# Value products over 128 rows for the last eight heads of a fused attention and feed-forward kernel

## The chip, the cores and the metric

The kernel runs on one core of a Trainium2 chip. The metric is the device time of one execution in microseconds (us), as a median of several runs. A core has a matrix engine (PE, with its weight loads shown as PEld), a vector engine (DVE), a scalar engine (ACT), a general engine (POOL) and an engine that mostly issues transfers (SP). Each works through its own queue in order; semaphores tie them together. Products are written to PSUM, eight banks of 512 f32 columns by 128 partitions; all else lies in SBUF.

## What is computed

The input x has 2048 rows of 512 columns. Part A is attention with 32 heads of 16 columns, in which a query sees itself and the 255 keys before it. Part B picks the 8 rows with the largest x @ w_r and adds a gated feed-forward result to them. The output mixes both by a gate for each row.

```python
qkv = x @ wqkv                              # 32 heads of 16
scores = einsum(q, k) * 16 ** -0.5          # mask: 0 <= i - j < 256
o = softmax(scores) @ v
a = o @ wo
r = x @ w_r;  idx = argsort(-r)[:8]
y = (silu(x[idx] @ w_gate) * (x[idx] @ w_up)) @ w_down
b = x;  b[idx] += y * sigmoid(r[idx])
out = g * a + (1 - g) * b                   # g = sigmoid(sum(x * gate_w))
```

## The kernel before

**Work and stages.** The 32 heads are four quarters c = 0 to 3 of eight heads, the 2048 rows are 16 row blocks j of 128 and 64 key blocks kb of 32. The scores are computed transposed: a product with the block-diagonal keys `Kbd` as weights and the queries `QT` as moving operand gives, for the 32 keys of one block, four heads on 128 partitions (head by key) and up to 256 query columns. The eight heads of a quarter are two sets s = 0, 1 of four heads; the products of set 0 use rows 0 to 63 of the PE array, those of set 1 rows 64 to 127 (`tile_position=(64 * s, 0)`), so that the two run side by side. One such group of score products is a *unit* (`unit`, L640 to L680): products at L658 into one of two pairs of banks of `psS`, an exponential on ACT at L669 that writes the weights `PT`, and a mask of the triangle at L680 on DVE or POOL. "M" units hold two key blocks, "T" units the last 32 query columns of eight. Quarters 0 and 1 go one after the other, 2 and 3 are interleaved by row block.

**Value products** (`pv`, L687). For each row block, key block and set s, `PT` (128 partitions of head and key, 128 queries) is the weight operand, and the values `Vbd` move. The 128 partitions are cut into halves r of two heads, one half a product of 64 rows and 34 columns (two heads of 16 values and a column of ones, which yields the softmax denominator), into bank r of `psO` (L699). `Vbd` has two buffers, one for c % 2 = 0 and one for 1. A value tile is made from a projection in `psG` (`v_tail`, L600): a transpose on DVE to the single buffer `VT` (L603) and two multiplications with a 0/1 column (L607, DVE or POOL) that put each head's values in its rows.

**Normalisation** (`norm`, L717). Of each batch of row blocks DVE takes the reciprocal of the denominators (L726), multiplies it with the gate (L738), and scales `psO` into `On` (L742). A DMA transposes `On` into `OT` (L772); for row blocks 14 and 15 of quarters 2 and 3 PE transposes it into a bank of `psG` (L759), and DVE (L767) or ACT (L764) copies it to `OT`. `outp` (L777) multiplies with `wo` (L793; L790 for blocks 14 and 15, over 128 rows), combines with (1 - g) * b on DVE (L798; block 15 adds it by a product, L785, and ACT copies, L796), and stores.

**Other work on PE.** Projections of q, k, v (L621, L628) into two banks of `psG`; gate and up products of the feed-forward part (L873, 112 products of 8 columns with weights in `big`), down products (L915, 14 products of 512 columns); a few filler products (L541, L545), which write nothing that is used.

**The end.** Every reciprocal is checked against limits, in two pieces of 480 and 32 columns (L1041 to L1043); two small products (L1048) sum the result, DVE writes `flag` (L1051), and all engines read it (L1182) and branch past a general version of the kernel (L1184).

**Order.** The order of every engine's queue is a table of numbers (`ORDER`, L1105; `BANK` and `FILL` beside it), one number for each operation in the order in which the program makes them. `Sched.schedule` puts the queues together by it and adds the waits. An operation that stands ahead in a queue and waits holds up all behind it.

## Time and profile before

| what | value |
|---|---|
| time before, median of 3 runs | 173.4 us (173.19 to 173.93) |
| the profiled execution | 172.88 us |
| its span, first to last instruction | 171.3 us |
| PE busy (modelled) | 157.3 us, 92%, 4575 products |
| DVE busy | 119.7 us, 70% |
| ACT busy | 138.3 us, 81% |
| POOL busy | 67.3 us, 39% |

In the groups of the profile each row has line, engine, operation, output and inputs, shapes and count; then busy us and mean ns of one; then the engine's idle time before these instructions, and what ended it. "64*128 64x34" is a product with a weight operand of 64 rows by 128 columns and 34 moving columns. In the timeline a row has start, length and count of like instructions that stand together. Products overlap in PE's pipeline: one lasts some 170 ns, but the next starts long before its end.

### The profile page before, as it was taken

How to read it: one execution, taken by the hardware profiler on the slowest of the kernel's cores; microseconds unless marked ns; L12 is line 12 of the kernel's file. 1: busy time of each engine (PE TensorE's matmuls, PEld its weight loads, DVE VectorE, ACT ScalarE, POOL GpSimd, SP SyncE). 2: the span in 40 equal slices, each digit the busy share in tenths (PEclk: the TensorE clock that was granted, in tenths of full speed). 3: DMA queues.
4: the chain of work that ended last, by engine and by line, in shares of the span. 5: the costliest groups of instructions: out<-in, count | busy, mean ns of one | idle time of the engine just before them, and what ended most of it. 6: DMA issues, size and time to landing. Idle time of an engine off the chain costs nothing. (4 is left out here: it accounts for less than half of the span.)

```text
span 171.3 us, 10022 instructions
## 1 busy us (share of the span) xinstructions
PE 157.3 (92%) x4575; PEld 108.2 (63%) x4575; DVE 119.7 (70%) x328; ACT 138.3 (81%) x171; POOL 67.3 (39%) x130
## 2 busy tenths in 40 slices
PE   4989999999999999999997999999999999689960
PEld 1447767766474776778783567576777587476520
DVE  7694899997684418687885756888974657568750
ACT  2277889999999879898999669999999989847120
POOL 2100364750793894202518143524353244246000
PEclk9999999999999957999999999999999999999997
DMA  6994194644677442440328532028110434424621
GB/s 131 216 229 104 18 247 84 154 108 110 154 188 125 125 84 65 139 136 13 96 72 151 188 64 67 4 67 159 32 65 4 103 90 127 122 88 109 188 86 53
DMA packets 35745, 18.68 MB, mean 109 GB/s; under 512 B 27616, under 2 KB 35568, under 8 KB 35568
## 3 DMA queue, kind: packets, MB, share of 16 engines
q1 hardware_dynamic: 34560, 17.71, 42.7%
q8 instruction: 36, 0.59, 1.5%
q10 hardware_dynamic: 1072, 0.26, 0.7%
q0 software_dynamic: 64, 0.02, 0.3%
q14 instruction: 13, 0.11, 0.2%
HBM read 11.81 MB, written 4.20 MB: 93 GB/s over the span
## 5 line engine op out<-in xcount | busy, mean ns | idle before, releaser
L669 ACT ACTIVATE f_PT<-f_psS 128x1024 bf16<-128x1024 f32 (+3 forms) x156 | 132.3, 918 | 16.2 <-PE f_psS L658 14.2
L680 POOL TENSOR_TENSOR f_PT<-f_PT,f_MK 128x128 bf16<-128x128 bf16 (+1 forms) x83 | 41.5, 513 | 83.7 <-ACT f_PT L669 79.8
L658 PE MATMUL f_psS<-f_QT,f_Kbd 64*128 64x256 bf16 (+3 forms) x960 | 65.4, 225 | 1.2 <-ACT f_PT L669 0.7
L628 PE MATMUL f_psG<-f_XT,f_W 64*128 64x512 bf16 x360 | 65.8, 379 | 0.3
L699 PEld LDWEIGHTS f_psO<-f_Vbd,f_PT 64*128 64x128 bf16 x2880 | 54.3, 93 | 10.3 <-DVE f_On L742 3.5
L699 PE MATMUL f_psO<-f_Vbd,f_PT 64*128 64x34 bf16 x2880 | 58.4, 174 | 2.2 <-DVE f_On L742 1.2
L658 PEld LDWEIGHTS f_psS<-f_QT,f_Kbd 64*128 64x128 bf16 x960 | 32.1, 94 | 19.1 <-ACT f_PT L669 10.6
L628 PEld LDWEIGHTS f_psG<-f_XT,f_W 64*128 64x128 bf16 x360 | 20.7, 93 | 9.9 <-PE f_psG L628 0.9
L793 PE MATMUL f_psG<-f_wo,f_OT 64*128 64x512 bf16 x112 | 22.9, 376 | 1.2 <-DVE f_outt L798 1.2
L680 DVE TENSOR_TENSOR f_PT<-f_PT,f_MK 128x128 bf16<-128x128 bf16 (+1 forms) x73 | 19.5, 285 | 4.7 <-ACT f_PT L669 4.5
L587 DVE TENSOR_SCALAR f_Kbd<-f_Kr,f_hm 128x512 bf16<-128x512 bf16 (+2 forms) x62 | 20.9, 374 | 1.9 <-ACT f_Kr L575 1.6
L798 DVE SCALAR_TENSOR_TENSOR f_outt<-f_xr,f_omg_f,f_psG 128x512 bf16<-128x512 bf16 x15 | 11.2, 744 | 8.6 <-PE f_psG L793 3.0
L575 DVE CAST f_QT<-f_psG 128x512 bf16<-128x512 f32 (+1 forms) x15 | 10.0, 664 | 6.9 <-PE f_psG L628 6.1
L603 DVE STREAM_TRANSPOSE f_VT<-f_psG 128x512 f32<-128x512 f32 x16 | 11.4, 712 | 3.3 <-PE f_psG L628 2.7
L607 POOL TENSOR_SCALAR f_Vbd<-f_VT,f_pb 128x512 bf16<-128x512 f32 x16 | 11.6, 729 | 2.5 <-DVE f_VT L603 2.3
L742 DVE TENSOR_TENSOR f_On<-f_psO,f_RG 128x512 bf16<-128x512 f32 (+1 forms) x17 | 11.2, 657 | 1.6 <-DMA f_OT<-f_On 1.1
L726 DVE RECIPROCAL f_RC<-f_psO 128x32 f32<-128x32 f32 (+1 forms) x17 | 5.8, 343 | 8.2 <-PE f_psO L699 8.1
L575 DVE CAST f_Kr<-f_psG 128x512 bf16<-128x512 f32 x12 | 8.2, 686 | 3.4 <-PE f_psG L628 3.2
L587 POOL TENSOR_SCALAR f_Kbd<-f_Kr,f_hm 128x512 bf16<-128x512 bf16 (+1 forms) x6 | 8.5, 1420 | 5.1 <-ACT f_Kr L575 5.1
L793 PEld LDWEIGHTS f_psG<-f_wo,f_OT 64*128 64x128 bf16 x112 | 7.6, 93 | 4.2 <-DVE f_outt L798 1.9
L607 DVE TENSOR_SCALAR f_Vbd<-f_VT,f_pb 128x512 bf16<-128x512 f32 x16 | 8.6, 549 | 0.1
L534 PE MATMUL f_psS<-f_RC 128*128 128x512 bf16 x10 | 3.9, 544 | 2.4 <-DVE f_pb L472 2.4
(106 smaller groups left out, 70.0 us busy)
## 6 DMA issues: line engine op xcount, KB each, us to landing
f_xc<-in_A_x_dram SPq DMA_DIRECT2D x8, 256.0 KB, 3.4
f_xr<-f_xc SPq DMA_DIRECT2D x16, 128.0 KB, 2.6
out_dram<-f_outt SPq DMA_DIRECT2D x16, 128.0 KB, 2.2
f_big<-in_B_w_gate_dram SPq DMA_DIRECT2D x8, 224.0 KB, 3.0
f_big<-in_B_w_up_dram SPq DMA_DIRECT2D x8, 224.0 KB, 3.6
f_OT<-in_B_w_down_dram SPq DMA_DIRECT2D x4, 256.0 KB, 3.8
f_W<-in_A_wqkv_dram SPq DMA_DIRECT2D x2, 384.0 KB, 3.9
f_xr<-in_B_w_down_dram SPq DMA_DIRECT2D x2, 256.0 KB, 4.1
```

The lines of the kernel that those rows point to most:

```text
L575: return e.copy(out=o, in_=i) if e is nc.scalar else e.tensor_copy(out=o, in_=i)
L587: add("dve", lambda e, h=h: e.tensor_scalar(out=Kbd[:, sl, a // 32:(a + n) // 32, h, :], in0=Kr[:, kr, a:a + n].rearrange("p (a k) -> p a ...
L603: add("dve", lambda e: e.transpose(out=VT[:], in_=psG[:, it.r, :]), item=it, w=[("VT", vb)], occ=630, due=due, cls="ev")
L607: add(VENG, lambda e, o=o, i=i, b=b: e.tensor_scalar(out=o, in0=i, scalar1=pb_[:, b:b + 1], scalar2=1.0, op0=ALU.mult, op1=ALU.mult), r=[( ...
L628: return e.matmul(psG[:, it.r, 0:n], W[P, kc, which, 128 * c:128 * c + 128], XT[P, kc, 512 * tc + a:512 * tc + a + n], start=(k8 == 0), st ...
L658: ins[s] = e.matmul(psS[:, sb2 + s, n * k:n * k + n], Kbd[P, kslot[(c, kb // 16)][0], kb % 16].rearrange("p h k -> p (h k)"), QT[P, c % 2, ...
L669: add("act", lambda e: e.activation(out=oa, in_=ia, func=ACT.Exp, scale=0.25), r=[("S", i % 2)], w=pk_ + [("ex", i)], occ=2 * nk * n * 0.8 ...
L680: add(eng, lambda e: e.tensor_tensor(out=v, in0=v, in1=m, op=ALU.mult), r=MKR + pk_, w=pk_, occ=cost[eng], due=at(i + 1), cls="mk", alt=(o ...
L699: ins[r] = e.matmul(psO[:, r, 68 * ji + 34 * s:68 * ji + 34 * s + 34], PT[P, s, o0:o0 + 128], Vbd[P, c % 2, s, kb, :], start=(kb == kbs[0] ...
L742: add("dve", lambda e: e.tensor_tensor(out=o, in0=i0_, in1=i1_, op=ALU.mult), r=["O", "RG"], w=[("On", ob, 0), ("On", ob, 1)], occ=60 + 12 ...
L793: return e.matmul(psG[:, it.r, :], OTrun(c, a, 1)[P], wo[P, c, :], start=(k8 == 0), stop=(k8 == 7), tile_position=(64 * x, 0), skip_group_ ...
L798: add("dve", lambda e: e.scalar_tensor_tensor(out=outt[:, xs, :], in0=xr[:, xs, :], scalar=omg_f[:, a:a + 1], in1=psG[:, it.r, :], op0=ALU ...
```

## The change

For quarter 3 alone (`FC = (3,)`) the value products use all 128 rows: `PT` of a set s, whole, is the weight operand, and 68 columns move (four heads of 16 values and a one), into bank s of `psO`. So one product takes the place of two. The value tiles are block-diagonal over four heads, and lie in `big`, where the gate and up weights lay, so they may be written once the gate and up products are done; a tile takes eight multiplications of half the size, four heads times two sets. The ones are written by two fills. The rows of `OT` for quarter 3 then have another order of heads, and the rows of `wo` are loaded accordingly, in two transfers for each of the four.

```diff
+        VF = [[...], [AP(big, 4352 * k, [[14336, 128], [68, 64], [1, 68]]) for k in (1, 2)]]
...
+            if c in FC:
+                for b in range(4):
+                    for s2 in range(2):
+                        add(VENG, lambda e, b=b, s2=s2: e.tensor_scalar(out=VF[c - 2][s2][:, 16 * tc:16 * tc + 16, 17 * b:17 * b + 16],
+                                                                        in0=VT[:].rearrange("p (k f) -> p k f", f=32)[:, :, 16 * s2:16 * s2 + 16],
+                                                                        scalar1=pf_[:, b:b + 1], scalar2=1.0, op0=ALU.mult, op1=ALU.mult),
+                            r=[("VT", vb), ("pf", b), ("Vfone", c, s2)], w=[("Vf", c, tc, b, s2)], occ=420, due=due + 2, cls="vb", alt=("dve", 290))
+                return
...
+        def pvf(c, j, ji, due, kbs):
+            for g in range(0, len(kbs), PVF):
+                part = kbs[g:g + PVF]
+                for s in range(2):
+                    def fn(e, s=s, part=part):
+                        ins = None
+                        for kb in part:
+                            o0 = poff(c, kb) + 128 * j - 32 * kb
+                            ins = e.matmul(psO[:, s, 68 * ji:68 * ji + 68], PT[:, s, o0:o0 + 128], VF[c - 2][s][:, kb], start=(kb == kbs[0]), stop=(kb == kbs[-1]), skip_group_check=True)
+                        return ins
...
+            if c in FC:
+                pvf(c, j, ji, due, kbs)
+                return
...
+PVF = 6
+FC = (3,)
```

The transposes of the last two row blocks go to the score banks (`psS`), block 14 to the first pair and block 15 to the second, no longer to `psG`. They are made at the end of the program, and each output product of these blocks now depends on its own quarter's part of `OT` alone.

```diff
-                it = S.item(None, True)
-
-                def fn(e):
-                    ins = None
-                    for ji in range(n):
-                        ins = e.matmul(psG[:, it.r, 128 * ji:128 * ji + 128], On[:, ob, ji, :], ident[:], start=True, stop=True)
-                    return ins
...
+                def late():
+                    k = j0 % 2
+
+                    def fn(e):
+                        ins = None
+                        for ji in range(n):
+                            ins = e.matmul(psS[:, 2 * k + (ji if k else 0), 128 * ji:128 * ji + 128], On[:, ob, ji, :], ident[:], start=True, stop=True, skip_group_check=True)
+                        return ins
...
+                    if k == 0:
+                        add("dve", lambda e: e.tensor_copy(out=OTrun(2, 14, 2), in_=psS[:, 0, 0:256]), r=[("S", 0)] + ow, w=[("OT", 2, 14), ("OT", 3, 14)], occ=70 + 266, due=due + 100, cls="nm")
+                    else:
+                        add("act", lambda e: e.copy(out=OTrun(2, 15, 1), in_=psS[:, 2, 0:128]), r=[("S", 1)] + ow, w=[("OT", 2, 15)], occ=55 + 107, lat=175 + 107, due=due + 100, cls="nm")
+                        add("dve", lambda e: e.tensor_copy(out=OTrun(3, 15, 1), in_=psS[:, 3, 128:256]), r=[("S", 1)] + ow, w=[("OT", 3, 15)], occ=70 + 133, due=due + 100, cls="nm")
...
-                add("pe", fn, r=[("OT", c, a) for c in ((k8 % 4,) if last else range(4))] + WO, item=it, occ=215, lat=380, due=due, half="f" if tail else 0, cls="op", cw=512 if tail else 256)
+                add("pe", fn, r=[("OT", c, a) for c in ((k8 % 4,) if tail else range(4))] + WO, item=it, occ=215, lat=380, due=due, half="f" if tail else 0, cls="op", cw=512 if tail else 256)
...
-FILL = {13: 33, 15: 3, 18: 1, 37: 33, 39: 1, 53: 17, 61: 1}
+FILL = {4: 1, 18: 1, 54: 33, 79: 1, 107: 1}
```

`ORDER`, `BANK` and `FILL` are new from the first row on, so the order differs in the whole kernel. Three places show it. First PE, in the dense stretch of quarters 2 and 3, before: L658 are scores, L699 value products, L793 output products with `wo`, of four score units in a row.

```order
L658 MATMUL f_psS<-f_QT,f_Kbd 128x256 x4
L793 MATMUL f_psG<-f_wo,f_OT 128x512
L699 MATMUL f_psO<-f_Vbd,f_PT 128x34 x32
L658 MATMUL f_psS<-f_QT,f_Kbd 128x256 x4
L793 MATMUL f_psG<-f_wo,f_OT 128x512 x8
L658 MATMUL f_psS<-f_QT,f_Kbd 128x32 x16
L699 MATMUL f_psO<-f_Vbd,f_PT 128x34 x32
L658 MATMUL f_psS<-f_QT,f_Kbd 128x256 x4
```

The same four units after the change: L679 are scores, L835 output products, L716 full-height value products.

```order
L679 MATMUL f_psS<-f_QT,f_Kbd 128x256 x4
L716 MATMUL f_psO<-f_big,f_PT 128x68 x24
L679 MATMUL f_psS<-f_QT,f_Kbd 128x256 x4
L835 MATMUL f_psG<-f_wo,f_OT 128x512 x8
L716 MATMUL f_psO<-f_big,f_PT 128x68 x24
L679 MATMUL f_psS<-f_QT,f_Kbd 128x32 x16
L835 MATMUL f_psG<-f_wo,f_OT 128x512
L679 MATMUL f_psS<-f_QT,f_Kbd 128x256 x4
```

The full-height products stand in blocks of 24 between lines that use half the rows: there are 16 such blocks, of 6 to 48 products. Second, PE at the down products (L915), before:

```order
L658 MATMUL f_psS<-f_QT,f_Kbd 128x32 x16
L699 MATMUL f_psO<-f_Vbd,f_PT 128x34 x56
L658 MATMUL f_psS<-f_QT,f_Kbd 128x256 x8
L915 MATMUL f_psG<-f_OT,f_HT 8x512 x8
L915 MATMUL f_psG<-f_xr,f_HT 8x512 x4
L915 MATMUL f_psG<-f_scr,f_HT 8x512 x2
L658 MATMUL f_psS<-f_QT,f_Kbd 128x256 x4
```

And after, where L957 are the down products and L739 the half-height value products:

```order
L679 MATMUL f_psS<-f_QT,f_Kbd 128x32 x16
L957 MATMUL f_psG<-f_OT,f_HT 8x512 x4
L679 MATMUL f_psS<-f_QT,f_Kbd 128x256 x8
L739 MATMUL f_psO<-f_Vbd,f_PT 128x34 x8
L957 MATMUL f_psG<-f_OT,f_HT 8x512 x2
L716 MATMUL f_psO<-f_big,f_PT 128x68 x4
L957 MATMUL f_psG<-f_OT,f_HT 8x512 x2
L716 MATMUL f_psO<-f_big,f_PT 128x68 x20
L679 MATMUL f_psS<-f_QT,f_Kbd 128x32 x16
L679 MATMUL f_psS<-f_QT,f_Kbd 128x256 x4
L957 MATMUL f_psG<-f_xr,f_HT 8x512 x4
L957 MATMUL f_psG<-f_scr,f_HT 8x512 x2
```

The 14 products stood in one piece, and now stand in four, with score units between. Third, the end of DVE's queue, before; `f_outt` are the output combinations, `f_scr` and `f_okc` the check of the denominators.

```order
L738 TENSOR_TENSOR f_RG<-f_RC,f_g_f 128x16
L1041 TENSOR_SCALAR f_scr<-f_RC 128x32
L742 TENSOR_TENSOR f_On<-f_psO,f_RG 128x2x2x64
L798 SCALAR_TENSOR_TENSOR f_outt<-f_xr,f_omg_f,f_psG 128x512
L767 CAST f_OT<-f_psG 128x256
L1042 SCALAR_TENSOR_TENSOR f_scr<-f_RC,f_scr 128x32
L798 SCALAR_TENSOR_TENSOR f_outt<-f_xr,f_omg_f,f_psG 128x512
L1043 TENSOR_REDUCE f_okc<-f_scr 128x1
L1051 TENSOR_SCALAR flag<-f_psO 1x1
```

After (L840 are the combinations, L1096 to L1098 the check, L1106 the flag):

```order
L1097 SCALAR_TENSOR_TENSOR f_scr<-f_RC,f_scr 128x32
L782 TENSOR_TENSOR f_On<-f_psO,f_RG 128x2x2x64
L840 SCALAR_TENSOR_TENSOR f_outt<-f_xr,f_omg_f,f_psG 128x512
L807 CAST f_OT<-f_psS 128x128
L840 SCALAR_TENSOR_TENSOR f_outt<-f_xr,f_omg_f,f_psG 128x512
L1098 TENSOR_REDUCE f_okc<-f_scr 128x1
L1096 TENSOR_SCALAR f_scr<-f_RC 128x480
L1097 SCALAR_TENSOR_TENSOR f_scr<-f_RC,f_scr 128x480
L1098 TENSOR_REDUCE f_okc<-f_scr 128x1
L1106 TENSOR_SCALAR flag<-f_psO 1x1
```

The three operations on 480 columns, which stood among earlier work, are now the last ahead of the flag.

78 lines of the change are left out of this document (52 added, 26 removed), and 132 rows, old and new, of the table ORDER.

## The prediction, on record before the changed kernel ran

> **What bounds the kernel now.** I read the page first, for the shares of the span.
>
> ```profile
> span 171.3 us, 10022 instructions
> PE 157.3 (92%) x4575; PEld 108.2 (63%) x4575; DVE 119.7 (70%) x328; ACT 138.3 (81%) x171; POOL 67.3 (39%) x130
> ```
>
> The profiled execution took 172.88 us, so 1.6 us lie around its span; it lies 0.5 us under the median of the runs, 173.4. PE's 92% is modelled time of pipelined products and says little, so I took the busy time by stretches (columns: PE, PEld, DVE, ACT, POOL), and in the dense stretch 100 to 140 us PE's and ACT's groups by form.
>
> ```profile
> 100.00:140.00 40.00, 39.61 (x1292) 27.86 (x1286) 28.57 (x69) 39.42 (x46) 15.43 (x30) 1.00 0.28 67
> 140.00:160.00 20.00, 17.68 (x595) 12.99 (x593) 13.72 (x33) 14.58 (x20) 8.93 (x17) 1.00 0.42 117
> ```
> ```profile
> L628 PE MATMUL f_psG<-f_XT,f_W 64*128 64x512 bf16 x102 | 19.4, 376 | 0.0
> L699 PE MATMUL f_psO<-f_Vbd,f_PT 64*128 64x34 bf16 x856 | 17.2, 174 | 0.2 <-DVE f_On L742 0.2
> L658 PE MATMUL f_psS<-f_QT,f_Kbd 64*128 64x256 bf16 x144 | 15.9, 270 | 0.1
> L793 PE MATMUL f_psG<-f_wo,f_OT 64*128 64x512 bf16 x46 | 11.2, 376 | 0.0
> L658 PE MATMUL f_psS<-f_QT,f_Kbd 64*128 64x32 bf16 x144 | 3.7, 174 | 0.0
> ```
>
> ACT (the exponentials, L669) is busy 39.4 of these 40 us. For PE's real load I need what one product costs in a run, from the first to the last start. The timeline of PE has runs of each kind (start, length, instructions):
>
> ```profile
> 57.72 1.34 PE L873 MATMUL f_psG<-f_xselT,f_big 128*128 128x8 bf16 x48 [0.35 <-issue]
> 58.99 0.39 PE L658 MATMUL f_psS<-f_QT,f_Kbd 64*128 64x256 bf16 x4
> ...
> 96.30 1.89 PE L915 MATMUL f_psG<-f_OT,f_HT 128*8 128x512 bf16 x8
> ...
> 99.84 0.75 PE L699 MATMUL f_psO<-f_Vbd,f_PT 64*128 64x34 bf16 x48
> 100.45 0.59 PE L628 MATMUL f_psG<-f_XT,f_W 64*128 64x512 bf16 x4
> ```
>
> ```profile
> L873 PE MATMUL f_psG<-f_xselT,f_big 128*128 128x8 bf16 x112 | 3.3, 167 | 0.3 <-issue 0.3
> ```
>
> A run of n takes one duration and n-1 steps. L915 (512 columns, 376 ns each as L628's) gives (1.89-0.376)/7 = 0.216 us for 512 columns, 0.42 ns a column. L699 gives (0.75-0.174)/47 = 12.3 ns, so the pair of 64-row products for one key block takes 24.6 ns. A 64-row product shares the array with the other half, so 512 columns cost 0.108 us and 256 cost 0.054. The stretch then holds 148 x 0.108 + 144 x 0.054 + 1000 x 0.0123 = 36.1 us of PE work in 40: ACT sets the pace, and PE has about 3.9 us left, some 10%. From 140 to 160 neither engine is full (17.7 and 14.6 of 20): there the waits of the closing blocks decide.
>
> **The end.** The chain of waits on the page is short, so I read the last instructions in the timeline and the line of the final branch (q marks a sequencer; min/median/max in ns).
>
> ```profile
> 162.39 0.42 DVE L742 TENSOR_TENSOR f_On<-f_psO,f_RG 128x256 bf16<-128x256 f32 x1
> 162.76 0.75 DVE L798 SCALAR_TENSOR_TENSOR f_outt<-f_xr,f_omg_f,f_psG 128x512 bf16<-128x512 bf16 x1
> 163.43 0.42 DVE L767 CAST f_OT<-f_psG 128x256 bf16<-128x256 f32 x1
> ...
> 165.03 0.75 DVE L798 SCALAR_TENSOR_TENSOR f_outt<-f_xr,f_omg_f,f_psG 128x512 bf16<-128x512 bf16 x1 [1.09 <-issue]
> 165.70 0.18 DVE L1043 TENSOR_REDUCE f_okc<-f_scr 128x1 f32<-128x32 f32 x1
> 166.23 0.15 DVE L1051 TENSOR_SCALAR flag<-f_psO 1x1 int32<-1x1 f32 x1 [0.35 <-PE f_psO L1048]
> ```
> ```profile
> 163.57 0.29 PE L759 MATMUL f_psG<-f_ident,f_On 128*128 128x128 bf16 x2 [0.68 <-DVE f_outt L798]
> 163.90 1.04 PE L790 MATMUL f_psG<-f_wo,f_OT 128*128 128x512 bf16 x4
> ...
> 164.99 1.03 PE L790 MATMUL f_psG<-f_wo,f_OT 128*128 128x512 bf16 x4
> 165.95 0.24 PE L1048 MATMUL f_psO<-f_ones_f,f_okc 128*1 128x1 f32 x4
> ```
> ```profile
> L1184 PEldq COMPARE_BRANCH  x1: 4133/4133/4133, 167.1 to 167.1; - x1
> ```
>
> The flag (L1051) is ready at 166.38, PE reads it and branches at 167.1, and that branch lasts 4.13 us, to 171.26: it is the span's last event. The last output's copy and store have ended before. So the end hangs on the flag, and the flag on DVE's check of the denominators.
>
> **The change part by part.** *Value products.* 720 half-height products of 34 columns, 720 x 12.3 ns = 8.9 us of PE, become 360 full-height ones of 68 columns. The trace has none of that shape. By L915's 0.42 ns a column one takes 28.7 ns; a little issue time on top makes 29 to 31, together 10.4 to 11.2 us. I take 10.9: +2.0 us of PE work, not a saving. The Trainium skill, page "TensorE: Matmul & The Clock Gate", Part 1, states that starts of successive products never come closer than about 25 ns, however few the columns; by that the old pair would take 50 ns and the edit would save 360 x 19 ns = 6.8 us. The row of 48 in 0.75 us shows 12.3 ns for products that alternate between the halves, so the trace disagrees and I go by the row.
>
> *Switches between 64 and 128 rows.* The first score product after the 48 L873 starts at 58.99, when the last of them, begun at 57.72+1.34-0.167 = 58.89, is only 0.07 us from its end: a step of 0.10 us. Between two half-height lines, L699 to L628 at 100.45, the last start was 100.42: 0.03 us. A switch lets the array run empty, for some 0.07 to 0.10 us. In PE's order, counted from the end of the gate and up products on, 3 switches become 37, around 16 blocks of full-height value products and the pieces of the down products: 34 x 0.09 = 3.1 us. With the products the second half gets +5.1 us of PE work (4.0 to 5.7). Its cover is PE's idle time under ACT, 3.9 us in 100 to 140, where by time some 3.3 of the 5.1 fall, and the idle time after 140. PE would then be at 39.4 of 40: as full as ACT, which waits for scores in the same queue. So not all of it can hide; but not all shows either. I take a quarter, **+1.3 us**, ends 0 and +5.1.
>
> *The first half* loses work: up to the end of the gate and up products 19 switches become 13, and 4 of 9 filler pieces of 240 columns (0.1 us each) go, some 0.9 us of PE in all. But ACT gets four evacuations of 512 Q columns for one and two of K for three, +2 x 0.586 us by
>
> ```profile
> L575 ACT CAST f_QT<-f_psG 128x512 bf16<-128x512 f32 x1 | 0.6, 586 | 0.2 <-PE f_psG L628 0.2
> ```
>
> These cancel as far as I can tell: **0**, ends -1.0 and +1.0.
>
> *The down products* stand in one piece before, 96.30 to 99.47, and ACT waits behind them:
>
> ```profile
> 99.87 1.51 ACT L669 ACTIVATE f_PT<-f_psS 128x1024 bf16<-128x1024 f32 x2 [1.57 <-PE f_psS L658]
> ```
>
> They are now in four pieces with scores between. PE's work is the same, so half of that wait may go: **-0.7**, ends 0 and -1.6.
>
> *Value tiles.* Eight multiplications a tile instead of two, at half the size: 8 before at 549 ns (DVE) or 729 (POOL), 32 after at no less than half of that.
>
> ```profile
> L607 POOL TENSOR_SCALAR f_Vbd<-f_VT,f_pb 128x512 bf16<-128x512 f32 x16 | 11.6, 729 | 2.5 <-DVE f_VT L603 2.3
> ...
> L607 DVE TENSOR_SCALAR f_Vbd<-f_VT,f_pb 128x512 bf16<-128x512 f32 x16 | 8.6, 549 | 0.1
> ```
>
> That is 17 x 0.3 + 15 x 0.4 = 11 us for 5, but over two engines at 28.6 and 15.4 of 40. Masks of 8 blocks move to POOL in exchange (DVE 20 to 14), so DVE keeps its load. What waits behind a tile is the next value transpose, which needs the single f_VT: nothing, ends 0 and +0.8. The two fills of ones on POOL and four more stores of f_wo on SP lie beside idle time: nothing.
>
> *The end.* The transposes of row block 15 no longer wait for a bank of f_psG (0.68 us), and two of block 14's products run ahead of them: after f_On (162.81) the transposes end near 163.2, two products of block 14 near 163.7, and the last L798 near 164.5 instead of 165.78, 1.3 us earlier. That f_On comes later by about 0.5: a second 32-column check stands ahead of it on DVE (0.18), the full-height block takes 0.15 longer than 48 pairs' worth, the transposes of block 14 stand in front (0.15). Against this, the three checks of 480 columns move from among the earlier work to the very end of DVE, behind the last L798:
>
> ```profile
> L1042 DVE SCALAR_TENSOR_TENSOR f_scr<-f_RC,f_scr 128x480 f32<-128x480 f32 x1 | 0.8, 762 | 0.0
> ...
> L1043 DVE TENSOR_REDUCE f_okc<-f_scr 128x1 f32<-128x480 f32 x1 | 0.6, 593 | 0.0
> ...
> L1041 DVE TENSOR_SCALAR f_scr<-f_RC 128x480 f32<-128x480 f32 x1 | 0.4, 403 | 0.0
> ```
>
> 1.76 us more ahead of the flag, of which 0.15 lay under PE's last products before: +1.6. Queued behind the flag is PE's long branch. Sum: +1.6 - 1.3 + 0.5 = **+0.8**, ends -0.8 (the branch is not the end after all, and the earlier store counts) and +1.3.
>
> **Sum.** 1.3 + 0 - 0.7 + 0 + 0.8 = +1.4 us: 174.3 against 172.88 of the profiled execution, **174.8** against the median.
>
> **The rivals.** *The new order recovers idle time (faster).* Before, ACT waits 14.2 us for scores in all,
>
> ```profile
> ACT f_PT L669 <- PE f_psS L658: 14.2, 21, 1.6
> ```
>
> and 4.8 of these lie after 140 us. If the other order closes 3 us of them and the extra PE work stays under ACT, the sum is -3 + 0.8 = -2.2: 171.2; with two of them 172.2. I give 0.32. Against it: at 98% real load in the dense stretch PE has little room to make up for anything. *Everything cancels* (0.26): PE's additional work stays hidden but for 0.5, the down products give 0.7, the end costs 0.5: 173.7. *Weights not hidden (much slower).* If each full-height weight load waits for the product in flight, 360 x 0.025 (L873's whole step of (1.34-0.167)/47 = 25.0 ns, load included) adds up to 9 us; with a third of that, +3, the total is 177.8. The Trainium skill, the same page, Part 3 (The mechanism), has such a rule: loads overlap products in flight only when the row groups differ. L873 loads 128 x 128 weights for every product in the same rows and still steps in 25 ns, so I give 0.05. *The quarter is too small (slower):* the score products come late in each block, and half of the 5.1 us shows, 1.3 more: 176.1; this is in the forecast's upper range.
>
> **How the numbers follow.** My forecast, slower by some 1.4 us, has 0.37, its own range 174.3 to 177.0. With the rival of weights slower has 0.42, no change 0.26, faster 0.32, taking 0.5% (0.87 us) as what a measurement of this kernel can tell. The range 171.2 to 177.2 leaves out the best part of the first rival and the worst of the third.
>
> **What would show it.** In the profile after: the full-height value products in steps of 29 to 31 ns; steps of 0.1 us at each switch; ACT's waits for scores longer between 100 and 140 us, and none of 1.5 us at the down products; the flag later after the last combination by about 1.7 us, and the branch of 4.1 us still last. Wrong it would be if ACT's waits shrink, if the products step in 25 ns or in over 40, or if the branch ends elsewhere.

## The result: slower by 3%, and the profile after

The changed kernel takes 178.76 us (median of 4 runs, 177.79 to 179.52) against 173.34 us (4 runs, 173.19 to 173.93) beside it: ratio 1.0303, 95% interval 1.0247 to 1.0359. On another chip it was 178.45 against 173.46 us, ratio 1.0270 (1.0227 to 1.0313). The profiled execution took 178.69 us with a span of 177.1, where the kernel before had 171.3: 5.86 us to explain, of which 1.4 were foretold. On most of the chips used below the runs of one kernel spread over several us, and the kernel before, loaded a second time, came out at 1.0113 of itself (1.0049 to 1.0178); so differences under about 1% are read from stages of the profiled executions, which mostly repeat between the 61st and the 141st exponential: the one from the 93rd to the 117th took 22.43 or 22.44 us in ten profiles with full-height products. From the 141st to the end of the last exponential they don't repeat: 16.87 and 18.06 us in the two profiles of the changed kernel.

The page after: the head of it, the costliest line of ACT, and the two lines of the full-height value products.

```profile
span 177.1 us, 9324 instructions
...
PE 160.7 (91%) x4208; PEld 108.3 (61%) x4209; DVE 124.8 (70%) x343; ACT 138.8 (78%) x173; POOL 77.1 (44%) x145
...
L690 ACT ACTIVATE f_PT<-f_psS 128x1024 bf16<-128x1024 f32 (+3 forms) x156 | 132.3, 919 | 19.4 <-PE f_psS L679 17.8
```
```profile
L716 PE MATMUL f_psO<-f_big,f_PT 128*128 128x68 bf16 x360 | 14.4, 194 | 0.0
L716 PEld LDWEIGHTS f_psO<-f_big,f_PT 128*128 128x128 bf16 x360 | 12.3, 97 | 4.4 <-issue 4.0 <-DVE f_Kbd L600 0.4
```

ACT does the same 132.3 us of exponentials and waits 19.4 us between them (16.2 before). Where it waits is seen in the table by stage, cut at the starts of the 1st, 53rd, 77th, 93rd, 117th, 121st and 141st exponential, the last one's end and the span's end. Each row: the stretch, its length, the time that exponentials took in it (those cut by a bound are counted in both), the TensorE clock granted, DMA. Before:

```profile
8.61:59.45 50.84, 44.92 (x52) 1.00 0.61 137
59.45:83.70 24.25, 20.45 (x25) 0.86 0.32 85
83.70:100.79 17.09, 13.74 (x16) 1.00 0.49 119
100.79:121.49 20.70, 20.50 (x25) 1.00 0.37 81
121.49:124.94 3.45, 3.35 (x5) 1.00 0.00 0
124.94:142.86 17.92, 17.25 (x21) 1.00 0.28 76
142.86:159.59 16.73, 12.11 (x17) 1.00 0.40 113
159.59:171.26 11.67, 0.00 (x0) 0.91 0.31 101
```

And after:

```profile
8.77:58.08 49.31, 44.43 (x53) 1.00 0.58 134
58.08:85.92 27.84, 20.91 (x25) 0.88 0.25 72
85.92:101.18 15.26, 13.14 (x17) 1.00 0.65 166
101.18:123.61 22.43, 20.95 (x26) 1.00 0.22 56
123.61:128.11 4.50, 3.37 (x6) 1.00 0.01 4
128.11:146.77 18.66, 17.26 (x21) 1.00 0.36 77
146.77:163.64 16.87, 12.21 (x17) 1.00 0.43 124
163.64:177.12 13.48, 0.00 (x0) 0.84 0.27 84
```

The differences of the lengths: -1.53, +3.59, -1.83, +1.73, +1.05, +0.74, +0.14 and +1.81 us; with the first exponential 0.16 later they make the 5.86. The stretch with the down products (77th to 93rd) became shorter, and the next one, in which 96 of the 360 full-height products stand, longer by about as much. The other large losses are the stretch around the gate and up products (53rd to 77th), four exponentials at 124 to 128 us, and the tail behind the last exponential.

### The profile page after: what moved, and what is told of

It is laid out like the page before. It is cut to its first block, busy times and chain, and to the rows that moved or that the text cites. A ratio compares the mean times of both kernels' runs of the same rounds, so it can differ in the third digit from the quotient of the medians.

```text
span 177.1 us, 9324 instructions
## 1 busy us (share of the span) xinstructions
PE 160.7 (91%) x4208; PEld 108.3 (61%) x4209; DVE 124.8 (70%) x343; ACT 138.8 (78%) x173; POOL 77.1 (44%) x145
## 4 chain that ended last, share of the span: by engine, by line
PE 64%; ACT 9%; DVE 9%; issue 7%; POOL 5%; DMA 2%; SPq 1%; POOLq 0%; DVEq 0%
PE f_psG L649 18%; PE f_psS L679 17%; PE f_psO L739 12%; ACT f_PT L690 8%; PE f_psO L716 6%; PE f_psG L835 6%; POOL f_PT L701 3%; DMA f_OT<-f_On 2%; PE f_psG L957 2%; PE f_psG L915 2%; DVE f_PT L530 1%; POOL f_big L1048 1%; DVE f_On L782 1%; DVE f_RG L778 1%; PE f_psG L861 1%
## 5 line engine op out<-in xcount | busy, mean ns | idle before, releaser
L690 ACT ACTIVATE f_PT<-f_psS 128x1024 bf16<-128x1024 f32 (+3 forms) x156 | 132.3, 919 | 19.4 <-PE f_psS L679 17.8
L701 POOL TENSOR_TENSOR f_PT<-f_PT,f_MK 128x128 bf16<-128x128 bf16 (+1 forms) x85 | 45.7, 553 | 69.8 <-ACT f_PT L690 69.6
L679 PE MATMUL f_psS<-f_QT,f_Kbd 64*128 64x256 bf16 (+2 forms) x960 | 65.4, 226 | 1.9 <-ACT f_PT L690 0.9
L649 PE MATMUL f_psG<-f_XT,f_W 64*128 64x512 bf16 x360 | 63.1, 378 | 0.1
L739 PE MATMUL f_psO<-f_Vbd,f_PT 64*128 64x34 bf16 x2160 | 45.7, 174 | 2.8 <-POOL f_PT L701 0.8
L739 PEld LDWEIGHTS f_psO<-f_Vbd,f_PT 64*128 64x128 bf16 x2160 | 41.9, 93 | 9.5 <-DVE f_On L782 2.6
L679 PEld LDWEIGHTS f_psS<-f_QT,f_Kbd 64*128 64x128 bf16 x960 | 31.4, 94 | 21.7 <-ACT f_PT L690 8.1
L701 DVE TENSOR_TENSOR f_PT<-f_PT,f_MK 128x128 bf16<-128x128 bf16 (+1 forms) x71 | 20.6, 305 | 11.1 <-ACT f_PT L690 10.9
L600 DVE TENSOR_SCALAR f_Kbd<-f_Kr,f_hm 128x512 bf16<-128x512 bf16 (+2 forms) x63 | 21.6, 381 | 1.8 <-ACT f_Kr L588 1.2
L835 PE MATMUL f_psG<-f_wo,f_OT 64*128 64x512 bf16 x112 | 21.1, 376 | 1.5 <-issue 0.9
L840 DVE SCALAR_TENSOR_TENSOR f_outt<-f_xr,f_omg_f,f_psG 128x512 bf16<-128x512 bf16 x15 | 11.2, 746 | 7.5 <-PE f_psG L835 3.8
L616 DVE STREAM_TRANSPOSE f_VT<-f_psG 128x512 f32<-128x512 f32 x16 | 11.4, 712 | 5.5 <-PE f_psG L649 5.3
L716 PEld LDWEIGHTS f_psO<-f_big,f_PT 128*128 128x128 bf16 x360 | 12.3, 97 | 4.4 <-issue 4.0
L716 PE MATMUL f_psO<-f_big,f_PT 128*128 128x68 bf16 x360 | 14.4, 194 | 0.0
L588 DVE CAST f_QT<-f_psG 128x512 bf16<-128x512 f32 (+1 forms) x12 | 7.8, 653 | 6.5 <-PE f_psG L649 6.4
L835 PEld LDWEIGHTS f_psG<-f_wo,f_OT 64*128 64x128 bf16 x112 | 7.0, 93 | 5.2 <-issue 1.2
L620 POOL TENSOR_SCALAR f_big<-f_VT,f_pf 128x256 bf16<-128x256 f32 x15 | 7.9, 541 | 1.6 <-DVE f_VT L616 1.5
```

The costliest lines, as they stand in the source:

```text
L588: return e.copy(out=o, in_=i) if e is nc.scalar else e.tensor_copy(out=o, in_=i)
L600: add("dve", lambda e, h=h: e.tensor_scalar(out=Kbd[:, sl, a // 32:(a + n) // 32, h, :], in0=Kr[:, kr, a:a + n].rearrange("p (a k) -> p a ...
L616: add("dve", lambda e: e.transpose(out=VT[:], in_=psG[:, it.r, :]), item=it, w=[("VT", vb)], occ=630, due=due, cls="ev")
L649: return e.matmul(psG[:, it.r, 0:n], W[P, kc, which, 128 * c:128 * c + 128], XT[P, kc, 512 * tc + a:512 * tc + a + n], start=(k8 == 0), st ...
L679: ins[s] = e.matmul(psS[:, sb2 + s, n * k:n * k + n], Kbd[P, kslot[(c, kb // 16)][0], kb % 16].rearrange("p h k -> p (h k)"), QT[P, c % 2, ...
L690: add("act", lambda e: e.activation(out=oa, in_=ia, func=ACT.Exp, scale=0.25), r=[("S", i % 2)], w=pk_ + [("ex", i)], occ=2 * nk * n * 0.8 ...
```

## The experiments

**The end: is it the checks?** *Checks early.* On DVE the three 480-column checks go from behind the last combination to between earlier ones:

```diff
- recip(15), check32, On(15), combine, combine, reduce32, check480 x3, flag
+ mask, check480, combine, check480, combine, check480, recip(14), ... combine, reduce32, flag
```

> The changed kernel with the three 480-column checks moved on VectorE from behind the last combination to the places between the combinations some 10 us earlier, where VectorE waits anyway. Theory (the checks hold the flag, and the branch behind the flag is the last event): the 1.7 us that the three take (0.40, 0.66 and 0.65 us) go from the end, 177.0 us, within 176.7 to 177.4. Rival (something else ends as late as the flag: the last store or TensorE's own queue): 178.4 to 178.8.

Measured: profiled run 176.90 us, span 175.2; ratio 1.0165 (1.0084 to 1.0246). The tail of DVE after, and then that of this run:

```profile
169.35 0.75 DVE L840 SCALAR_TENSOR_TENSOR f_outt<-f_xr,f_omg_f,f_psG 128x512 bf16<-128x512 bf16 x1 [0.45 <-DMA f_xr<-f_xc]
...
170.11 0.40 DVE L1096 TENSOR_SCALAR f_scr<-f_RC 128x480 f32<-128x480 f32 x1
...
170.55 0.66 DVE L1097 SCALAR_TENSOR_TENSOR f_scr<-f_RC,f_scr 128x480 f32<-128x480 f32 x1
171.24 0.65 DVE L1098 TENSOR_REDUCE f_okc<-f_scr 128x1 f32<-128x480 f32 x1
...
172.22 0.15 DVE L1106 TENSOR_SCALAR flag<-f_psO 1x1 int32<-1x1 f32 x1 [0.33 <-PE f_psO L1103]
```
```profile
168.90 0.75 DVE L840 SCALAR_TENSOR_TENSOR f_outt<-f_xr,f_omg_f,f_psG 128x512 bf16<-128x512 bf16 x1
...
170.25 0.15 DVE L1106 TENSOR_SCALAR flag<-f_psO 1x1 int32<-1x1 f32 x1 [0.52 <-PE f_psO L1103]
```

From the last combination's end to the flag's it is 2.27 us after and 0.75 here; from the last exponential's end to the span's end 13.48 and 11.59, about as in the kernel before (11.67). The branch on PE stays the last event.

*The kernel before with the checks late*, the one edit the other way round:

> The kernel before with one thing of the change: the three 480-column checks stand on VectorE behind the last combination and ahead of the flag. Theory (the flag and the branch behind it are the end): from the last exponential's end to the span's end 11.7 us become 13.3 to 13.5, the time 174.9 to 175.2 us against 173.3. Rival (the 1.7 us are hidden in the kernel before): 173.2 to 173.6 us.

Measured: ratio 1.0045 (0.9932 to 1.0157), which tells nothing; TensorE fell to half clock in the tail of the profiled execution (14.27 us of tail). The step itself can be read, since it is DVE's: from the combination's end to the flag's end 168.22 to 170.49, 2.27 us, where the kernel before has 0.59 (165.78 to 166.37).

```profile
167.47 0.75 DVE L798 SCALAR_TENSOR_TENSOR f_outt<-f_xr,f_omg_f,f_psG 128x512 bf16<-128x512 bf16 x1 [1.80 <-issue]
...
170.34 0.15 DVE L1051 TENSOR_SCALAR flag<-f_psO 1x1 int32<-1x1 f32 x1 [0.33 <-PE f_psO L1048]
```

So the checks cost 1.5 us in the changed kernel (2.27 less 0.75) and 1.7 us in the kernel before.

**58 to 86 us: the fills of ones.** GpSimd after, in the timeline: a fill (L1048) stands ahead of masks (L701); the second fill, at 70.54 us, does too.

```profile
66.61 1.28 POOL L1048 CAST f_big<-f_pf 128x256 bf16<-128x256 f32 x1
...
67.95 2.64 POOL L701 TENSOR_TENSOR f_PT<-f_PT,f_MK 128x128 bf16<-128x128 bf16 x3
```

And PE's waits from 58 to 86 us, after:

```profile
PE f_psO L739 <- POOL f_PT L701: 0.8, 2, 0.6
PE f_psO L739 <- DVE f_PT L701: 0.7, 1, 0.7
```

All three, 1.5 us, are waits for masks. Two are for masks of GpSimd, behind the fills in its queue. The third is for a mask of DVE, which no fill holds:

```profile
75.17 1.28 DVE L701 TENSOR_TENSOR f_PT<-f_PT,f_MK 128x128 bf16<-128x128 bf16 x1
```

It lies beside a GpSimd mask of 1.14 us (75.23 to 76.37), one of those that came later because of the fills, and ends 0.08 us behind it. In the run with fills and tile moved the same DVE mask took 0.29 us. So a fill here also did harm by what it pushed beside DVE's work. Three places were tried for the fills:

```diff
  POOL: ... mask | fill | copy, masks | fill | copy, masks, tiles, masks (76.4) | idle 2.6 | tile, mask (80.4) | 68-column tile
- fills at both first bars
+ fills_later: at "idle 2.6";  fills_80: ahead of the 68-column tile
+ fills_and_tile: as fills_80, and DVE's first 68-column tile behind four key tiles
```

> The changed kernel with the two fills of ones (1.28 us each on GpSimd, at 66.6 and 70.5 us) moved behind the mask that ends at 76.4 us, into 2.6 us in which GpSimd has nothing to do. Theory (the fills hold masks, for which the value products and with them the scores wait): the 69th exponential starts 1.5 to 2.5 us sooner and the end comes 1 to 2 us sooner, 176.8 to 177.8 us. Rival (the loss of 3.8 us between the 53rd and the 69th exponential comes from TensorE's own work being put later, or from the half clock): 178.5 to 179.0 us.

> The changed kernel with the two fills of ones put behind the mask that ends at 80.4 us on GpSimd, ahead of the first 68-column value tile, where GpSimd then has 6.8 us with nothing to do. Theory (at 66.6 and 70.5 us the fills hold three masks, 1.55 us of gaps on TensorE; put into the 2.6 us behind the mask of 76.4 us, as the experiment before did, they only held the next value tile, and TensorE waited 1.36 us there): both waits are gone, TensorE has no gap over 0.3 us between 60 and 90 us but the one at the router, the 73rd exponential starts 1.2 to 1.6 us sooner against the 53rd, and the end comes about as much sooner, 177.2 to 177.6 us. Rival (GpSimd is so full up to the 92nd exponential that the 2.6 us cost the same wherever they stand): 178.5 us or more.

> The changed kernel with the fills of ones behind 80.4 us on GpSimd, as in the run before, and with VectorE's first 68-column value tile moved behind four key tiles, so that VectorE does not stand waiting for the fill (1.9 us there) with a key copy behind it, for which TensorE waited 1.37 us. Theory (what a fill costs is what is queued behind it or behind its reader): now both waits are gone; against the changed kernel, measured from the 61st exponential, the 77th comes 1.2 to 1.7 us sooner and stays so to the 117th; the end 1 to 1.6 us sooner on equal clocks. Rival (the stretch up to the 92nd exponential is bound otherwise): 0.3 us or less at the 77th.

Lengths from the 61st to the 69th, 73rd and 81st exponential, after, and then with fills and tile moved (fills_later 8.35, 5.75 and 7.14; fills_80 8.26, 3.88 and 8.76):

```profile
68.51:78.31 9.80, 7.55 (x9) 1.00 0.44 120
78.31:82.32 4.01, 3.32 (x4) 1.00 0.15 48
82.32:89.47 7.15, 5.96 (x10) 1.00 0.20 50
```
```profile
67.98:76.22 8.24, 7.21 (x9) 1.00 0.43 113
76.22:80.10 3.88, 3.35 (x6) 1.00 0.36 114
80.10:87.66 7.56, 6.06 (x10) 1.00 0.21 45
```

In all three runs the first stretch is about 1.5 us shorter: the masks' waits are gone. The first two places gave it back, in the second and in the third stretch: the sum is 20.96 us after, 21.24 and 20.90 there, and their theories fell. Nor do their times show a gain (fills_later: median 181.15 us, ratio 1.0251, 1.0152 to 1.0350; fills_80: median 181.3 us, no interval). In the run with three moves below, the fills stood as in fills_80; its waits from 78 to 86 us on DVE, and PE's from 58 to 86, say what gave it back:

```profile
DVE f_big L620 <- POOL f_big L1048: 1.9, 1, 1.9
```
```profile
PE f_psG L649 <- DVE f_Kr L588: 1.4, 1, 1.4
```

DVE stands at a value tile that needs the fill, a key copy waits behind it, and PE for the bank that the copy frees. With that tile moved too the sum is 19.68, 1.28 us less, the gain is still there at the 141st exponential (1.27), and the profiled run took 176.07 us (ratio 1.0094, 0.9975 to 1.0214). A fill costs what is queued behind it, or behind its reader, and what it pushes beside another engine's work.

**124 to 128 us: one transpose.** After, in the timeline of DVE and PE: a value projection sits in a PSUM bank until DVE's transpose (L616) has read it, and that stands behind key tiles (L600), one of which took 1.24 us. PE's output product (L835) needs the bank.

```profile
123.12 1.24 DVE L600 TENSOR_SCALAR f_Kbd<-f_Kr,f_hm 128x512 bf16<-128x512 bf16 x1
...
124.27 0.70 DVE L616 STREAM_TRANSPOSE f_VT<-f_psG 128x512 f32<-128x512 f32 x1
...
125.19 0.37 PE L835 MATMUL f_psG<-f_wo,f_OT 64*128 64x512 bf16 x1 [0.90 <-issue]
```

That tile is most of the delay. Where the transpose was moved (below) it found its projection ready at 122.87 us, with all of this 0.48 us earlier than after; so after, the projection was ready near 123.35 (an estimate), and a third tile of the usual 0.35 us would have held the transpose some 0.1 us. The long tile lies beside a GpSimd mask of 1.20 us, from 123.00 on.

```diff
- DVE: key copy, key tile, key tile, key tile (1.24), transpose, key tile
+ DVE: key copy, key tile, key tile, transpose, key tile, key tile
```

> The changed kernel with one instruction moved on VectorE: the transpose that frees a PSUM bank for the output products at 125.2 us stands ahead of two of the four key tiles that it stood behind (one of them took 1.23 us). Theory (TensorE's gap of 0.90 us there, and ScalarE's wait of 1.13 us behind it at the 119th exponential, come from this order and from no work of the products): both go, and with TensorE short of slack behind it the end comes 0.6 to 1.0 us sooner, 177.8 to 178.2 us. Rival (the time lost is made up or taken by the next wait anyway): no change, 178.6 to 178.9 us.

The edit moves the transpose past one tile only, the long one. Measured, from the 117th to the 121st exponential 3.59 us for 4.50, the whole difference from before but 0.14:

```profile
123.13:126.72 3.59, 3.37 (x6) 1.00 0.02 5
```

No tile was long in that run (three took 1.11 us), so it does not part the order from the long tile. In this one profile the end kept less: of the 0.91 us the last exponential had 0.07 left, where a combination waited 1.3 us for the store of an earlier output, and the span's end 0.55. Since that stretch differs by 1.2 us between two profiles of one kernel, what reaches the end is not settled. Median 178.1 us, beside 176.68 for the kernel before on that chip (172.14 to 177.11, no interval).

**The products themselves.** *Half-height products in the last quarter*, from the same tiles. All key blocks of one set now come ahead of the other set's; with full height the sets take turns, six key blocks each:

```diff
-            for g in range(0, len(kbs), PVF):
-                part = kbs[g:g + PVF]
-                for s in range(2):
+            for s in range(2):
+                for g in range(0, len(kbs), PVF):
+                    part = kbs[g:g + PVF]
...
-                            ins = e.matmul(psO[:, s, 68 * ji:68 * ji + 68], PT[:, s, o0:o0 + 128], VF[c - 2][s][:, kb], ...)
+                            for r in range(2):
+                                P = slice(64 * r, 64 * r + 64)
+                                ins[r] = e.matmul(psO[:, r, 68 * ji + 34 * s:68 * ji + 34 * s + 34], PT[P, s, o0:o0 + 128], VF[c - 2][s][P, kb, 34 * r:34 * r + 34], ...)
```

> The changed kernel with the last quarter's value products made again as alternating half-height ones of 34 columns (720 for 360), from the same value tiles, in the same place in the order; the row order of the output weights goes with it. The full-height products' extra work on TensorE goes (360 x 32.2 ns for 720 x 12.3 ns, 2.7 us, and 34 switches of about 0.09 us, 3.1 us: 5.8 us in all). Theory (between the 93rd exponential and the last TensorE has no slack, so the extra work shows nearly whole): the loss of 3.7 to 4.5 us there goes, 174.2 to 175.2 us. Rival of the prediction (a quarter of it shows): 177.2 to 177.6 us. Second rival (it is the order of the rest, not this work): 178.4 us or more.

Measured: ratio 1.0272 (1.0191 to 1.0353), no gain to be seen. By stage, from the 93rd, 117th, 121st and 141st exponential on (the rows of the changed kernel stand above), and PE's wait in the first of these stretches:

```profile
103.48:126.02 22.54, 20.79 (x25) 1.00 0.28 56
126.02:130.38 4.36, 3.36 (x6) 1.00 0.01 4
130.38:147.94 17.56, 17.12 (x22) 1.00 0.42 80
147.94:168.71 20.77, 12.10 (x17) 0.84 0.45 104
```
```profile
PE f_psO L718 <- POOL f_PT L701: 0.7, 1, 0.7
```

Up to the 141st exponential the halves bring 1.13 us, nearly all in the third row, where ACT then does 17.12 us of exponentials in 17.56. My first theory (3.7 to 4.5 us) fell: ACT sets the pace there, and the other waits stay. In the first row the halves bring nothing, but there they have a wait of their own. After its first 12 value products of a row block PE stands 0.65 us (at 108.53) until a GpSimd mask is done; with full height the first 12 products run through at the same place (106.08), since the other set's are next. All five profiles with half-height products have this wait, so they understate what the products cost. Behind the 141st exponential TensorE was at half clock for a part, and 3.9 us were lost. *With the checks early as well*:

> The changed kernel with half-height products in the last quarter (as tried alone before) and with the 480-column checks between the combinations (as tried alone before), to be set against the changed kernel with the checks alone (span 175.2 us). Theory A (the extra TensorE work shows nearly whole): 3 to 4 us less than with the checks alone, a span of 171.2 to 172.2 us. Theory B, formed on the run before, in which half-height products brought only 1.1 us from the 93rd to the 141st exponential (ScalarE sets the pace there, and waits of the new order stay, such as 1.1 us at the 119th): 1 to 2 us less, a span of 173.2 to 174.2 us.

Measured: span 176.7 us (median 178.72), where the checks alone had 175.2; the 141st exponential again 1.19 us sooner, and again a half-clock stretch behind it. Up to there theory B held; the end fitted neither theory.

*34 of the 68 columns*, with the sets in turns as in the changed kernel, parts columns from switches:

> The changed kernel with only 34 of the 68 columns in each full-height value product of the last quarter: the sums of the other four heads of each eight are left out, all 360 products, their weights and all 50 switches stay. It parts columns from switches. Theory (columns 2.7 us and switches 3.1 us, both shown nearly whole): a product comes down from 32.2 ns to between 17 and 25 ns, 2.6 to 5.5 us less work, of which three quarters show: 174.8 to 176.8 us, with the drain at each switch still 0.1 us longer than a plain step. Rival (the price of a product is its weights or its start, not its columns): the step stays over 30 ns and the time at 178.3 us or more.

Measured: profiled run 175.90 us, median 177.66, ratio 1.0125 (1.0013 to 1.0237). A block of 48 in PE's timeline, after, and here, each with the line behind it:

```profile
155.59 1.70 PE L716 MATMUL f_psO<-f_big,f_PT 128*128 128x68 bf16 x48
157.22 0.39 PE L679 MATMUL f_psS<-f_QT,f_Kbd 64*128 64x256 bf16 x4
```
```profile
153.10 1.38 PE L716 MATMUL f_psO<-f_big,f_PT 128*128 128x34 bf16 x48
154.41 0.28 PE L679 MATMUL f_psS<-f_QT,f_Kbd 64*128 64x256 bf16 x2
```

A product of 68 columns steps in (1.70 - 0.194) / 47 = 32.0 ns, one of 34 in (1.38 - 0.178) / 47 = 25.6: halving the columns takes 20% off. Behind the block the next line starts 0.12 us after the last product's start (155.59 + 47 x 0.03204 = 157.10), 0.09 more than a step: the switch as foretold. The stages from the 93rd and from the 121st exponential on:

```profile
100.91:122.95 22.04, 20.90 (x25) 1.00 0.23 57
127.42:144.93 17.51, 17.11 (x22) 1.00 0.31 82
```

The 360 x 6.4 ns = 2.3 us less of work brought 1.57 us by the 141st exponential (44.02 us from the 93rd on for 45.59), more than the halves, which take away 5.8 us of work but have the wait for the mask. By the last exponential's end it is 2.70 us, of which 1.1 come from the stretch that does not repeat.

**Adding up.** *Three moves* (checks early, fills as in fills_80, transpose first):

> The changed kernel, its full-height products and value tiles as they are, with three moves in the order of VectorE and GpSimd: the 480-column checks between the combinations, the fills of ones behind 80.4 us, and the transpose ahead of two key tiles. If the three costs add up (1.8 us, 1.4 us and 0.8 us): a span of 173.1 us against 177.1, 174.8 us, still 1.0 to 1.5 us slower than the kernel before. If the gaps only move from one place to the next: 176.5 to 177.0 us.

Measured: span 175.2, median 176.62 us. The first exponential came 1.3 us later than after; of the moves the fills gave nothing, as above. The expected 174.8 was missed by 0.4. *Four moves* (with fills_and_tile in place of fills_80), with full-height and with half-height products, twice:

> The changed kernel, its full-height products as they are, with four moves in the order: checks between the combinations (1.8 us), fills behind 80.4 us with the first 68-column tile behind the key tiles (1.2 to 1.6 us), the transpose ahead of two key tiles (0.9 us at the 119th exponential, of which the output blocks behind the 141st took back part). Theory (the loss is mostly these waits of the order): a span of 172.8 to 174.0 us where the changed kernel had 177.1 and the kernel before 171.3. Rival (the full-height products' extra work holds the end whatever the order): 175 us or more.

> The same four moves with half-height products in the last quarter. If the products' extra work costs the 1.2 us by the 141st exponential that the two runs before showed, the 141st comes 1.0 to 1.4 us sooner than with full-height products under the same moves; if the output blocks set the pace behind it, the end gains less than that. A span of 171.5 to 173 us on equal clocks, about the kernel before; were the extra work the main loss after all, 170 us or less.

> The four moves with full-height products once more: within 0.5% of the kernel before, 4 to 5 us less than the changed kernel; no half-clock stretch between the 93rd and the last exponential, as in the eight traces with full-height products so far.

> The four moves with half-height products once more. If half-height products as such bring TensorE to half clock late in the kernel (three of three traces had one or two stretches of 3.4 us behind the 141st exponential): again such a stretch, and no less time than with full-height products. If those were chance: no stretch, and 1 to 2 us less than with full-height products, 0.5 to 1% faster than the kernel before.

Full height: spans 173.6 and 174.6; 0.9977 (0.9887 to 1.0068) on a chip where the kernel before spread from 173.97 to 178.52, and 1.0150 (1.0111 to 1.0190) on the one where it did not, 176.11 us beside 173.46. The second, narrower interval counts: the moves bring 2.3 us of the 5.0 by the medians on that chip (178.45 to 176.11), and a loss of 1.5% stays; my expectation of "within 0.5%" was a miss. Half height: 1.0003 (0.9892 to 1.0115), and 177.63 us, with runs from 173.08 (mean clock 0.988) to 179.16 (0.955). The 141st exponential came 1.1 us sooner than with full height, as expected (the stage from the 121st: 17.51 for 18.74), and all of it was lost behind. In the run of 173.08 us the mean clock leaves room for some 4.1 us at half clock in all, and the stretch near 60 us, which every trace has, takes at least 3.4 of them. So that run, which was not profiled, probably had no late stretch; it lies 2.5 us under the fastest run with full height on that chip (175.62). The second half-height profile from the 141st exponential on, and PE's wait there:

```profile
144.66:165.96 21.30, 12.30 (x17) 0.84 0.36 104
```
```profile
PE f_psG L838 <- DVE f_outt L843: 2.4, 1, 2.4
```

PE waits 2.4 us (145.84 to 148.28) for a bank that a combination must free. That combination stands 3.8 us idle, and the profile shows no releaser; that it waits for a transfer is a guess. TensorE's clock is halved from 147.77 for 6.8 us.

*Both kernels once more, on that chip:*

> The changed kernel as it is, once more, beside the next three on one chip: 1.5 to 3.5% slower than the kernel before, and no half-clock stretch of TensorE behind the 141st exponential but the last one at the very end.

> The kernel before as it is, for a second profile: its last quarter has half-height products too. If these bring the half clock, a stretch of 3.4 us of it lies between the 93rd exponential and the end, which the first profile did not have; if not, the only stretch is the one that begins near 60 us.

After: 1.027, as given above, with no late stretch. The kernel before, with its half-height products, had none between the 93rd exponential and its end either. *Key copy to VectorE*, a fifth move, with either height:

```diff
- ACT: exponentials, key copy (106.3), exponentials;  DVE: key tiles, key tile
+ ACT: exponentials;  DVE: key tiles, key copy, key tile
```

> The four moves with full-height products, and the key copy that ScalarE makes at 106.3 us moved to VectorE, which waits for it there anyway. Theory (ScalarE sets the pace between the 93rd and the 117th exponential, so its 0.5 us of copy show): the 117th exponential, measured from the 93rd, comes 0.5 us sooner (22.43 us become 21.9), and the end as much: about 2.0 us slower than the kernel before, 1.0 to 1.3%. Rival (TensorE is behind there too): 0.2 us or less.

> The five moves with half-height products. Runs without a half-clock stretch in the last 30 us: 172.5 to 173.2 us, 0.2 to 0.5% faster than the kernel before; with one, 175 us and more. If half-height products bring such a stretch in this order, as in four of four profiles, the profile has it behind the 141st exponential and the median is at 175 us or more.

Measured, from the 93rd to the 117th exponential: 22.51 us, where the four moves had 22.43. ACT's 0.6 us of copy became 0.6 us more of waiting for PE (2.0 for 1.4): the theory fell, its rival held. Ratio 1.0104 (1.0028 to 1.0179); with half height 1.0063 (0.9986 to 1.0139), 173.75 to 179.0 us (median 176.8), and again a half-clock stretch (156.25, for 3.4 us). No version was shown to beat the kernel before.

## Why the prediction was right in direction and too small

Forecast +1.4 us, measured +5.9 in the profiled execution, outside the range. The direction was no luck: the two terms that made it, the products and the end, are there. Term by term:

*Value products and switches, +1.3.* The sizes nearly held (32 ns a product for 29 to 31, 0.09 us more at a switch as foretold). The share did not: "I take a quarter", but with half of the columns gone 1.57 of 2.3 us of work came back by the 141st exponential, two thirds. Half-height products brought 1.1 to 1.2 of 5.8 us by there, held back by their own wait of 0.65 us for a mask. So the term was too small: by the 141st exponential the columns alone are 1.6 us; how much the switches add, and what all of it costs behind the 141st exponential, is open: no half-height profile got through there at full clock.

*Value tiles: "the two fills of ones on POOL ... lie beside idle time: nothing".* This step failed: 1.3 us. I read GpSimd's share of busy time over 40 us and not what is queued behind the fill. There were masks behind it, PE behind the masks, and one of the late masks lay beside a mask of DVE that then took 1.28 us. "Masks of 8 blocks move to POOL in exchange" had no price either: GpSimd has 14 masks of 128x512 after and had 8 before, and both slow DVE instructions (this one and the tile at 123.12) lie beside such a mask.

*"What waits behind a tile is the next value transpose ...: nothing, ends 0 and +0.8".* This failed too. The transpose came late once, behind key tiles and not behind value tiles, one of them slow beside GpSimd, and that cost 0.9 us at 124 us. I had the right instruction and looked for the wait in the wrong place; DVE's order showed it.

*The end, +0.8.* Measured +1.8. The checks were right (+1.6 foretold, 1.5 to 1.7 measured). "1.3 us earlier" for the transposes in the score banks was 0.9 (from the end of `f_On` to the last combination's end 2.97 us before and 2.05 after), and "f_On later by about 0.5" was 1.2 (from the last exponential's end 3.23 before, 4.41 after). I had counted what stands directly ahead of it on DVE. PE too was late: it began the 48 half-height products ahead of the last output block 0.48 us behind the last exponential's end (164.12), where the kernel before began such a block 0.14 us ahead of that end (159.45).

*First half 0, down products -0.7.* From the first exponential to the 77th the changed kernel lost 2.1 us, of which the fills explain 1.3. The stretch of the down products did become shorter, by 1.83 us, though 4 of the 14 products moved out of it, and no wait of 1.5 us is left there, as foretold. The 1.73 us that the next stretch lost were not foretold as such. PE is busy there without a gap, before and after, and by the steps above its added work is some 3 us (an estimate: 1.0 for 11 switches, 1.1 for value products, 0.9 for the four down products). Half of the columns gave 0.4 us back; the rest was not parted. Part of the +3.59 between the 53rd and the 77th is only work put later: in the 16 exponentials from the 53rd on PE makes 112 gate and up products where it made 64 before, and the 53rd had come 1.5 us sooner. ACT's extra key copy, which I had counted as a cost, cost nothing where it was tried (106.3 us).

Of the rivals, "weights not hidden" is refuted: the loads take 97 ns each and the products step in 32. That speaks against the rule of the Trainium skill, "TensorE: Matmul & The Clock Gate", Part 3 (The mechanism), that loads overlap only in other row groups; the same section also has loads pulled ahead into a background weight buffer, and no trace here tells whether that is the case. "The new order recovers idle time" went the wrong way: moves in the order alone brought back 2.3 of the 5.0 us. "The quarter is too small" was right for the columns, and its 176.1 still fell short, for the waits of the order came on top. No run had the full-height products in the old order, so the two were never parted as wholes.

## What to carry to other kernels

An instruction beside idle time of its engine is free only if nothing that a later engine needs stands behind it in the queue: follow the queue at that place, not the engine's share, and see what the delayed instructions then lie beside. When an edit comes with a new order, cost the order: list the producers of PSUM banks and masks that PE waits for, and what stands ahead of each. And a stage saved upstream of a chain of transfers is not yet a gain at the end: the same 1.1 us was reached in five profiles, and in all five the stretch behind took longer (18.6 to 21.3 us, where eleven profiles with all columns at full height have 16.1 to 18.1).

## What the runs showed of the hardware

*The clock may fall after short waits.* In the five profiles with half-height products in the new order there are six half-clock stretches behind the 141st exponential, each 3.41 or 6.83 us, and each began within 1.2 us of the end of a gap of 1.5 to 2.4 us on PE. Twelve with full-height products had no stretch there but the one at the very end, and no gap over 0.91 us up to the last exponential; the kernel before had a gap of 1.20 us (148.61) and no stretch. That the gap brings the half clock is inferred, not tried, and it is not the whole rule: the kernel before with late checks has a stretch at 165.82 us behind gaps of 0.54 and 0.68 us only, and the stretch at 60 us, in every trace, has no PE gap over 0.5 us just ahead of it in the first profiles of both kernels. The Trainium skill, the same page, Part 1 (What's actually happening), gives windows of 3413 ns, which the lengths bear out, and an idle window of about 3.4 us ahead of the fall, which they don't.

*Full-height products did not step closer than 25 ns*: 8 columns take 25.0, 34 take 25.6 and 68 take 32.0, while the kernel's alternating half-height ones of 34 start every 12.3.

*DVE can be held as long as a GpSimd instruction lasts.* A key tile of 128x512 takes 0.35 us where GpSimd does nothing (41 of them after). Of 14 that lie beside GpSimd's work for over half of their time 13 took 0.35 to 0.57 us, and the one at 123.12 took 1.24 us: it ended 0.16 us behind a GpSimd mask of 1.20 us. The DVE mask at 75.17 took 1.28 us and ended 0.08 us behind a GpSimd mask of 1.14 us. The long mask is in all seven profiles of the changed order with the fills in their place and in none with the fills moved, the long tile in all nine without the moved transpose and in none with it. Why some are held and others not, the traces don't show.
